# Retention attention into a mixture of experts: another order of the last attention tile, of its index load and scatters, and of the work behind them

## The chip, the cores and the metric

One NeuronCore of a Trainium2 chip runs the whole program in one launch. The metric is the device time of one execution in microseconds, the median over several executions. Shorter is better.

## What is computed

A block-wise retention attention over 4 sequences, 8 heads, 768 positions and 64 channels, whose output is regrouped into 3072 token rows of 512 numbers. Each row goes to one of 8 experts, the one with the largest gate logit.

```python
def _attn_ref(q, k, v, lam):
    ...
    for b in range(nb):
        ...
        intra = np.einsum('bhic,bhjc->bhij', qb, kb) * Dmask[None]
        intra = np.einsum('bhij,bhjd->bhid', intra, vb)
        inter = np.einsum('bhid,bhde->bhie', qb * lam_pow[None], kv_state)
        out[:, :, sl] = intra + inter
        kv_state = lam_block[None, :, None, None] * kv_state + np.einsum('bhsd,bhse->bhde', kb_dec, vb)

def _moe_ref(x, w_gate, w_output_gate, w1, w2):
    logits = x @ w_gate
    e_idx = np.argmax(logits, axis=1)
    ...
    for e in range(E):
        h = np.maximum(x[mask] @ w1[e], 0.0)
        out[mask] = gate_w[mask, None] * eom[mask, e, None] * (h @ w2[e])
```

## The kernel before

The attention part walks over 24 tiles (`NTILE`): 6 blocks of 128 positions by 4 sequences (`B`). `LAST` is 20, the first tile of the last block. Of each tile n, TensorE makes transposes of keys and queries (`pk`, `pq`), scores (`ps`, `stage_b`), the products of the scaled queries with the running state (`po`, `stage_c1`, line 424) and the products of the decayed scores `at` with the values, summed into the same `po` (`stage_c`, line 441). The scaled queries `qd` are made on GpSimd (line 375), in two halves for the last block. ScalarE copies `po` to `xT`, VectorE turns `xT` to token rows `xn` and SyncE writes them to the DRAM tensor `x_d` (`stage_d2`).

After each block of four tiles the gate logits are made (`logits`, `logit_rows`), VectorE chooses the expert (`route_choose`) and the place of each token in its expert's list (`route_place`), and GpSimd scatters a record of three numbers for each token to the DRAM table `tab_d` (`place_scatter`, one indirect DMA for each tile). Reading a list back (`load_rows`, the index) gives the rows to gather (`row_index`, then `gather`, one indirect DMA for 32 tokens, on GpSimd).

The expert part takes the experts by size, the first one (index 0 here) being picked early. Each expert's two weight matrices come in four pieces of 1 MB, 0 and 1 of `w1`, 2 and 3 of `w2`; piece 4 is the first of the next expert. `load_piece` issues one on SyncE's queue; there are three buffers, so a piece waits until the piece three before it has been split. A split makes a high part `whi` on ScalarE (`split_hi`) and a low part `wlo` on VectorE (`split_lo2`, line 146, two chunks of 128 rows at a time). Each product is the sum of three (`mm3`, lines 85 to 87).

The first expert's work starts while the last tiles are still being placed. Its first 192 rows (`FIRST`) are known early; its up products for them (`up_mm`, `ph`) and its down products (`down_rows_mm`, `pyr`) are cut into units, which `fill(count)` issues on TensorE between the steps of the last block. `settle` issues the activations that belong to units already made. Rows from place 352 on (`LATE`) belong to the last block's tokens; they aren't gathered but picked out of token rows on chip (`rows_of` transposes them, `mark_late` and `take_late` make the tile `chosen`, `split_late` splits it). Behind the units comes the second column half, `up(0, fc, 1)`, for columns 192 to 448, then the down products of the rest, then expert 1.

Instructions stand in the order in which the code is written, engine by engine, and each engine and each queue takes its own in that order. The waits between them are put in from the tiles that they share; DRAM tensors count as tiles.

## Time and profile before

| what | us |
|---|---|
| median of 3 runs | 416.05 (414.84 to 416.11) |
| the profiled execution: time | 415.14 |
| its span | 413.4 |
| TensorE busy in the span | 400.8 |
| VectorE, GpSimd, ScalarE busy | 286.7, 238.8, 190.4 |

The profile is that of one execution. Times in it are microseconds from the start of the span. The granted clock of TensorE is 1.00 of full speed in every stretch that is read here. TensorE's last products of the attention part start at 112.76, the first product of the experts at 116.83.

### The profile page before, as it was taken

Reading aid. Unit: us, or ns where it says so; the run is one execution under the profiler, and the core shown is the slowest. Engines: PE = TensorE matmul, PEld = TensorE weight load, DVE = VectorE, ACT = ScalarE, POOL = GpSimd, SP = SyncE. Lnnn points to the kernel's source line nnn. Section 1 sums busy time; section 2 is a strip of 40 time slices with the busy share of each in tenths; the row PEclk is TensorE's granted clock in tenths of the full one; section 3 lists DMA queues with packets and bytes.
Section 4 is the critical chain, followed back from the end, with each engine's and each line's share of the span. In section 5 each row is a group of like instructions: output and inputs, shape, how many; then the busy total and the mean of one; then the engine's idle time right before and its main releaser. Section 6 shows DMA issues by size and latency. Waiting matters only on the chain.

```text
span 413.4 us, 10570 instructions
## 1 busy us (share of the span) xinstructions
PE 400.8 (97%) x3869; PEld 367.1 (89%) x3869; DVE 286.7 (69%) x810; ACT 190.4 (46%) x460; POOL 238.8 (58%) x301
## 2 busy tenths in 40 slices
PE   7999999999899999999999999999999999999994
PEld 4889878798698698999999999999999989989983
DVE  2759697877888646876868857957965864873710
ACT  4767665665684033544145325504704543542400
POOL 5367679668846788674783665467386266120012
PEclk9999999999999999999999999999999999999999
DMA  8999898889972764544479548746846884461001
GB/s 177 231 254 246 226 258 224 215 230 259 322 231 79 222 206 144 170 141 135 150 209 297 198 135 241 262 178 200 292 140 186 295 271 151 127 224 46 5 27 52
DMA packets 95103, 79.11 MB, mean 191 GB/s; under 512 B 58445, under 2 KB 70769, under 8 KB 95041
## 3 DMA queue, kind: packets, MB, share of 16 engines
q1 hardware_dynamic: 88080, 64.88, 53.2%
q0 software_dynamic: 6240, 12.93, 10.0%
q8 instruction: 32, 0.52, 0.5%
q10 hardware_dynamic: 720, 0.53, 0.5%
q14 instruction: 31, 0.25, 0.2%
HBM read 62.25 MB, written 16.45 MB: 190 GB/s over the span
## 4 chain that ended last, share of the span: by engine, by line
PE 85%; DVE 6%; DMA 5%; issue 2%; POOL 1%; ACT 0%; POOLq 0%; DVEq 0%; SPq 0%
PE ph_None L86 10%; PE ph_None L87 10%; PE ph_None L85 10%; PE py L87 6%; PE py L86 6%; PE py L85 6%; PE pyr L86 5%; PE pyr L87 5%; PE pyr L85 5%; PE ps L400 4%; PE po L441 4%; PE pk L341 3%; PE po L424 2%; PE pq L341 2%; DVE at L409 2%; PE pst L454 2%
## 5 line engine op out<-in xcount | busy, mean ns | idle before, releaser
L900 POOL DMA_INDIRECT xg<-x_d,rows x100 | 110.6, 1106 | 54.8 <-issue 28.9
L1009 ACT ACTIVATE hhi<-ph_None 128x400 fp32r<-128x400 f32 (+4 forms) x56 | 28.1, 501 | 115.8 <-PE ph_None L87 111.0
L86 PE MATMUL ph_None<-xlo,whi 128*128 128x400 f32 (+4 forms) x224 | 76.2, 340 | 0.0
L87 PE MATMUL ph_None<-xhi,wlo 128*128 128x400 f32 (+4 forms) x224 | 76.1, 340 | 0.0
L85 PE MATMUL ph_None<-xhi,whi 128*128 128x400 f32 (+4 forms) x224 | 76.1, 340 | 0.0
L132 ACT CAST whi<-raw 128x512 fp32r<-128x512 f32 x128 | 74.7, 615 | 2.4 <-DMA raw<-in_moe_w_dram 2.4
L141 DVE TENSOR_TENSOR wlo<-raw,whi 128x512 fp32r<-128x512 f32 x112 | 74.5, 686 | 0.7 <-ACT whi L132 0.5
L1010 DVE SCALAR_TENSOR_TENSOR hlo<-ph_None,hhi 128x400 fp32r<-128x400 f32 (+4 forms) x56 | 31.9, 570 | 35.2 <-ACT hhi L1009 33.2
L87 PE MATMUL py<-hhi,wlo 128*128 128x400 f32 (+2 forms) x128 | 44.4, 347 | 0.0
L86 PE MATMUL py<-hlo,whi 128*128 128x400 f32 (+2 forms) x128 | 44.4, 347 | 0.0
L85 PE MATMUL py<-hhi,whi 128*128 128x400 f32 (+2 forms) x128 | 44.4, 347 | 0.0
L86 PEld LDWEIGHTS ph_None<-xlo,whi 128*128 128x128 f32 x224 | 42.0, 188 | 0.5 <-DVE xlo L935 0.2
L1126 POOL DMA_INDIRECT out_dram<-yn,table x12 | 12.5, 1045 | 51.8 <-DVE yn L1190 34.6
L85 PEld LDWEIGHTS ph_None<-xhi,whi 128*128 128x128 f32 x224 | 42.0, 188 | 0.4
L87 PEld LDWEIGHTS ph_None<-xhi,wlo 128*128 128x128 f32 x224 | 42.0, 188 | 0.2
L345 ACT COPY qT<-pq 64x256 f32<-64x256 f32 x96 | 37.8, 393 | 2.0 <-PE pq L341 1.0
L409 DVE TENSOR_TENSOR at<-ps,decay 128x512 f32<-128x512 f32 x48 | 31.1, 681 | 10.4 <-PE ps L400 10.4
L86 PE MATMUL pyr<-wlo,hhi 128*128 128x512 f32 (+2 forms) x96 | 37.8, 394 | 0.5 <-DVE wlo L146 0.5
L87 PE MATMUL pyr<-whi,hlo 128*128 128x512 f32 (+2 forms) x96 | 37.6, 391 | 0.0
L85 PE MATMUL pyr<-whi,hhi 128*128 128x512 f32 (+2 forms) x96 | 37.5, 390 | 0.0
L931 ACT CAST xhi<-y 128x256 fp32r<-128x256 f32 (+3 forms) x64 | 19.5, 357 | 31.5 <-DVE y L917 31.5
L679 POOL DMA_INDIRECT tab_d<-rec,idx x24 | 26.2, 1090 | 10.0 <-issue 4.1
(216 smaller groups left out, 783.0 us busy)
## 6 DMA issues: line engine op xcount, KB each, us to landing
raw<-in_moe_w_dram SPq DMA_DIRECT2D x32, 1024.0 KB
x_d<-xn SPq DMA_DIRECT2D x22, 256.0 KB
qkv<-in_k_dram SPq DMA_DIRECT2D x40, 128.0 KB
qkv<-in_v_dram SPq DMA_DIRECT2D x20, 256.0 KB
qkv<-in_q_dram SPq DMA_DIRECT2D x36, 128.0 KB
yd<-yo SPq DMA_DIRECT2D x12, 256.0 KB
yr<-yd SPq DMA_DIRECT2D x48, 64.0 KB
xg<-x_d,rows POOLq DMA_INDIRECT x100
```

Of the source, the lines that this page charges most:

```text
L85: nc.tensor.matmul(ps, a[0], b[0], start=first, stop=False)
L86: nc.tensor.matmul(ps, a[0], b[1], start=False, stop=False)
L87: nc.tensor.matmul(ps, a[1], b[0], start=False, stop=last)
L132: nc.scalar.copy(out=hi, in_=src)
L141: eng.tensor_tensor(out=lo, in0=src, in1=hi.bitcast(F32), op=ALU.subtract)
L341: nc.tensor.transpose(out=dst[:, m * P : (m + 1) * P], in_=src[:, m], identity=ident)
L345: copies = [lambda r=r, view=view, src=src: nc.scalar.copy(out=view(qT[r]), in_=src) for r, view, src in query_parts(pq)]
L409: nc.vector.tensor_tensor(out=at, in0=ps.rearrange("p (g t) -> p g t", g=NPAIR), in1=dec[:, j], op=ALU.mult)
L679: nc.gpsimd.indirect_dma_start(out=tab_d, out_offset=bass.IndirectOffsetOnAxis(ap=idx, axis=0), in_=rec, in_offset=None, bounds_check=P * ...
L900: nc.gpsimd.indirect_dma_start(out=xg[(p, i)][:, m * P : (m + 1) * P], out_offset=None, in_=x_q[0 : 4 * rows], in_offset=bass.IndirectOffs ...
L1009: nc.scalar.activation(out=hi[:, r], in_=ph[:, r], func=AF.Relu)
L1010: nc.vector.scalar_tensor_tensor(out=lo[:, r], in0=ph[:, r], scalar=0.0, in1=hi[:, r].bitcast(F32), op0=ALU.max, op1=ALU.subtract,)
```

## The change

All of it lies between the end of the attention part and the first expert. For the last tile (23) the products of scores and values go ahead of those of the state (`stage_last` in place of `stage_c1` and `stage_c`), and the row transposes of tiles 20 and 21 stand between the two, in banks of the tile's own scores. The up units start with columns 0 and 1 interleaved (first their first two input chunks, then the others), two units are issued ahead of the choice and six more behind it, eight ahead of the counts where there were four. The index load for the first expert's middle places moves from GpSimd to SyncE (`load_middle`, which reads only places below 352), and the last four scatters are declared free of it. Piece 3's load stands behind it on the queue. The first low half of piece 2 and `sort_rest` stand ahead of the first expert's second `row_index`; `stage_d2` of the last three tiles and `split_late` move behind the low parts of piece 3; piece 4's load stands ahead of the index of expert 1.

```diff
--- before.py
+++ after.py
@@ -297,6 +297,7 @@
         norow = wpool.tile([P, E * EB * 3], I32, tag="raw", bufs=3, name="norow")
         nc.gpsimd.memset(norow, NOROW)
         nc.sync.dma_start(tab_d.rearrange("(p r) t -> p (r t)", p=P), norow)
+        nc.gpsimd.memset(middle_t, NOROW)
 
 
     later = []
@@ -404,7 +405,8 @@
     def stage_b2(n):
         L = live[n]
         dec = decay.rearrange("p (y m) t -> p y m t", y=2)
-        for j, ps in enumerate(L.pop("ps")):
+        L["kept"] = L.pop("ps")
+        for j, ps in enumerate(L["kept"]):
             at = slot(f"at_{n}_{j}").rearrange("p (g t) -> p g t", g=NPAIR)
             nc.vector.tensor_tensor(
                 out=at, in0=ps.rearrange("p (g t) -> p g t", g=NPAIR), in1=dec[:, j], op=ALU.mult
@@ -428,6 +430,39 @@
                             start=(i == 0),
                             stop=False,
                         )
+
+    def stage_last(n, between):
+        L = live[n]
+        b = n % B
+        vt = qkv[n][2]
+        ps = L["kept"]
+        L["po"] = [bank(f"po_{n}_{y}") for y in range(2)]
+        for y in range(2):
+            for m in range(4):
+                i, j = divmod(m, 2)
+                nc.tensor.matmul(
+                    L["po"][y][j * D : (j + 1) * D, i * P : (i + 1) * P],
+                    vt[:, 4 * y + m, :],
+                    L["at"][y][:, m, :],
+                    start=(i == 0),
+                    stop=False,
+                )
+        copies = between(ps)
+        for i in range(2):
+            for y in range(2):
+                for j in range(2):
+                    r = slice(y * D, (y + 1) * D)
+                    nc.tensor.matmul(
+                        L["po"][y][j * D : (j + 1) * D, i * P : (i + 1) * P],
+                        state[b][r, 2 * i + j, :],
+                        L["qd"][r, 2 * i + j, :],
+                        start=False,
+                        stop=(i == 1),
+                    )
+        xT = L["xT"] = xTs[n] = slot(f"xT_{n}")
+        for y in range(2):
+            nc.scalar.copy(out=xT[:, 256 * y : 256 * y + 256], in_=L["po"][y][:, 0:256])
+        return copies
 
     def stage_c(n):
         L = live[n]
@@ -488,9 +523,10 @@
     spaces = {}
     xTs = {}
 
-    def logits(n0, nb):
+    def logits(n0, nb, pl=None):
         parts = P // EG // nb
-        pl = bank(f"pl_{n0}")
+        if pl is None:
+            pl = bank(f"pl_{n0}")
         for i in range(NPAIR // parts):
             for b in range(nb):
                 xTv = xTs.pop((n0 + b)) if i == NPAIR // parts - 1 else xTs[n0 + b]
@@ -671,20 +707,23 @@
 
     pending = []
 
-    def place_scatter(count):
+    def place_scatter(count, beside=()):
         for _ in range(min(count, len(pending))):
             idx, rec = pending.pop(0)
-            scatter(
-                "table",
-                nc.gpsimd.indirect_dma_start(
-                    out=tab_d,
-                    out_offset=bass.IndirectOffsetOnAxis(ap=idx, axis=0),
-                    in_=rec,
-                    in_offset=None,
-                    bounds_check=P * E * EB - 1,
-                    oob_is_err=False,
-                ),
-            )
+            ins = nc.gpsimd.indirect_dma_start(
+                out=tab_d,
+                out_offset=bass.IndirectOffsetOnAxis(ap=idx, axis=0),
+                in_=rec,
+                in_offset=None,
+                bounds_check=P * E * EB - 1,
+                oob_is_err=False,
+            )
+            scatter("table", ins)
+            for other in beside:
+                tc.declare_no_dep(
+                    getattr(ins, "ins", ins), other,
+                    reason="the first expert's places below LATE are read, the last tiles' places begin at LATE",
+                )
 
     def scatter(group, ins):
         inst = getattr(ins, "ins", ins)
@@ -834,6 +873,18 @@
         eng.dma_start(t, src.rearrange("e (b r) j t -> (e r) b (j t)", b=4))
         idxs[(p, j0)] = (t, n)
 
+    middle_t = const.tile([32, 4, 2, 3], I32, name="index_0_1")
+
+    def load_middle():
+        parts = []
+        idxs[(0, 1)] = (middle_t, 2)
+        for j in range(2):
+            nb = min(4, (LATE - P * (j + 1)) // 32)
+            src = tab_v[bass.ds(expert[0], 1)][:, 0 : 32 * nb, 1 + j : 2 + j, :]
+            ins = nc.sync.dma_start(middle_t[:, 0:nb, j, :], src.rearrange("e (b r) j t -> (e r) b (j t)", b=nb))
+            parts.append(getattr(ins, "ins", ins))
+        return parts
+
     def load_outs(p, j0=0, j1=None):
         if p >= E:
             return
@@ -941,13 +992,14 @@
 
     token_rows = {}
 
-    def rows_of(n):
+    def rows_of(n, pt=None):
         xT = live[n]["xT"]
-        pt = bank(f"pt_{n}")
+        if pt is None:
+            pt = bank(f"pt_{n}")
         for g in range(NPAIR):
             nc.tensor.transpose(out=pt[:, g * P : (g + 1) * P], in_=xT[:, g * P : (g + 1) * P], identity=ident)
         t = token_rows[n] = slot(f"xr_{n}")
-        nc.scalar.copy(out=t, in_=pt)
+        return lambda: nc.scalar.copy(out=t, in_=pt)
 
     chosen = []
 
@@ -1194,10 +1246,11 @@
 
     units = []
     acts = []
-    for fc in range(NFC):
-        for kc in range(NKC):
-            act = (lambda fc=fc: up_act(0, fc, 0)) if kc == NKC - 1 else None
-            units.append((lambda fc=fc, kc=kc: up_mm(0, fc, 0, kc), act))
+    for fc, kc in [(f, c) for h in range(2) for f in range(2) for c in (2 * h, 2 * h + 1)] + [
+        (f, c) for f in range(2, NFC) for c in range(NKC)
+    ]:
+        act = (lambda fc=fc: up_act(0, fc, 0)) if kc == NKC - 1 else None
+        units.append((lambda fc=fc, kc=kc: up_mm(0, fc, 0, kc), act))
     for j in range(2):
         for fc in range(NFC):
             act = (lambda j=j: emit_rows(0, j, phs.pop((0, "y", j)))) if fc == NFC - 1 else None
@@ -1344,33 +1397,34 @@
         for f in held[6:]:
             f()
         place_scatter(B)
-        load_rows(0, 1, 3, nc.gpsimd)
+        middle = load_middle()
         stage_c(n - 1)
         for g in range(NPAIR):
             x_hi(0, g, 0)
         for g in range(NPAIR):
             x_lo(0, g, 0)
         split_lo2(0, 0)
+        load_piece(3)
+        copies = stage_last(n, lambda free: [rows_of(LAST + i, free[i]) for i in range(2)])
+        pl = bank("pl_last")
+        copies.append(rows_of(LAST + 2))
         split_hi(0, 2)
-        load_piece(3)
-        stage_c1(n)
-        stage_c(n)
         split_hi(0, 3)
         split_lo2(0, 1)
-        for i in range(2):
-            rows_of(LAST + i)
-        logits(LAST, B)
-        rows_of(LAST + 2)
+        logits(LAST, B, pl)
+        copies.append(rows_of(LAST + 3))
+        for f in copies[:3]:
+            f()
         for j in range(2):
             split_hi(1, j)
+        copies[3]()
+        fill(2)
         logit_rows(LAST)
         choose = route_choose(LAST, NTILE)
-        at_once(choose[:-1])
-        rows_of(LAST + 3)
-        choose[-1]()
+        at_once(choose)
         for j in range(2, 4):
             split_hi(1, j)
-        fill(4)
+        fill(6)
         place = route_place(LAST, NTILE)
         counts = rank_counts("pcount")
         place[0]()
@@ -1381,32 +1435,34 @@
         fill(4)
         take_late(LAST)
         at_once(place[4:])
-        place_scatter(B)
+        place_scatter(B, middle)
         settle()
         for h in range(2):
             split_lo2(1, h)
         for j in range(4):
             split_hi(2, j)
+        split_lo2(2, 0)
+        sort_rest(counts)
         row_index(0, 1)
         gather(0, 6, 11, LAST * P)
-        stage_d2(LAST + 1)
-        stage_d2(n - 1, 2)
-        split_late()
-        sort_rest(counts)
         expert_regs(1, order_i[:, 1:2], 1)
+        load_piece(4)
         load_rows(1)
-        load_piece(4)
         load_outs0()
         expert_regs(2, order_i[:, 2:E], E - 2)
         for h in range(2):
             split_hi(3, 2 * h)
             split_hi(3, 2 * h + 1)
             fill(8)
-            split_lo2(2, h)
             settle()
+            if h == 0:
+                split_lo2(2, 1)
         for h in range(2):
             split_lo2(3, h)
             fill(2)
+        stage_d2(LAST + 1)
+        stage_d2(n - 1, 2)
+        split_late()
         row_index(1)
         gather(1, 0, 4)
         settle()
```

On TensorE, the last tile's products before: `po_23` are the two halves of the output of tile 23, `pt` the transposed rows, `pl` the logits, `at` the decayed scores.

```order
L424 MATMUL po_23_0_2599<-qkv_23_1_2119,state_1_140 64x128 x2
L424 MATMUL po_23_1_2600<-qkv_23_1_2119,state_1_140 64x128 x2
L424 MATMUL po_23_0_2599<-qkv_23_1_2119,state_1_140 64x128 x2
L424 MATMUL po_23_1_2600<-qkv_23_1_2119,state_1_140 64x128 x2
L441 MATMUL po_23_0_2599<-at_23_0_2536,qkv_23_1_2119 64x128 x4
L441 MATMUL po_23_1_2600<-at_23_1_2538,qkv_23_1_2119 64x128 x4
L948 MATMUL pt_20_2622<-ident_101,xT_20_2396 128x128 x4
L948 MATMUL pt_21_2629<-ident_101,xT_21_2493 128x128 x4
L501 MATMUL pl_20_2636<-xT_20_2396,wgs_107 32x128
```

The same place with the change:

```order
L443 MATMUL po_23_0_2600<-at_23_0_2538,qkv_23_1_2121 64x128 x4
L443 MATMUL po_23_1_2601<-at_23_1_2540,qkv_23_1_2121 64x128 x4
L1000 MATMUL ps_23_0_2520<-ident_101,xT_20_2398 128x128 x4
L1000 MATMUL ps_23_1_2521<-ident_101,xT_21_2495 128x128 x4
L455 MATMUL po_23_0_2600<-qkv_23_1_2121,state_1_140 64x128 x2
L455 MATMUL po_23_1_2601<-qkv_23_1_2121,state_1_140 64x128 x2
L455 MATMUL po_23_0_2600<-qkv_23_1_2121,state_1_140 64x128 x2
L455 MATMUL po_23_1_2601<-qkv_23_1_2121,state_1_140 64x128 x2
L1000 MATMUL pt_22_2632<-ident_101,xT_22_2570 128x128 x4
L537 MATMUL pl_last_2631<-xT_20_2398,wgs_107 32x128
```

The four rows with `state` have moved behind the score products and behind the transposes of `xT_20` and `xT_21`.

On SyncE's queue, from the write of tile 20's rows (`xn_20`) to piece 5, before (`raw` are pieces, `index_1` and `table_0` read `tab_d`, the `ISA` rows set registers):

```order
L534 DMA x_d_72<-xn_20_2475 128x512
...
L119 DMA raw_3_2597<-in_moe_w2_dram 128x4x512
L534 DMA x_d_72<-xn_21_2839 128x512
L534 DMA x_d_72<-xn_22_2842 128x2x512
L738 TENSOR_LOAD order_i_152
L738 ISA x2
...
L834 DMA index_1_0_2870<-tab_d_73 32x4x12
...
L119 DMA raw_4_2872<-in_moe_w1_dram 128x4x512
...
L738 TENSOR_LOAD order_i_152
L738 ISA x12
...
L119 DMA raw_5_3048<-in_moe_w1_dram 128x4x512
```

And with the change:

```order
L570 DMA x_d_72<-xn_20_2477 128x512
...
L884 DMA index_0_1_157<-tab_d_73 32x4x3
...
L884 DMA index_0_1_157<-tab_d_73 32x3x3
...
L119 DMA raw_3_2598<-in_moe_w2_dram 128x4x512
L777 TENSOR_LOAD order_i_152
L777 ISA x2
...
L119 DMA raw_4_2873<-in_moe_w1_dram 128x4x512
...
L873 DMA index_1_0_2875<-tab_d_73 32x4x12
...
L777 TENSOR_LOAD order_i_152
L777 ISA x12
L570 DMA x_d_72<-xn_21_3026 128x512
L570 DMA x_d_72<-xn_22_3029 128x2x512
```

Piece 3 now stands behind two index loads, and the writes of tiles 21 to 23 (`xn_21`, `xn_22`) behind piece 4, the index of expert 1, the tables and the second register load.

On VectorE, from the low parts of piece 1 on, before:

```order
L146 TENSOR_TENSOR wlo_1_2663<-raw_1_2299,whi_1_2662 128x1024 x2
L869 SCALAR_TENSOR_TENSOR rowf_0_1_2815<-index_0_1_2566 32x8
L874 TENSOR_SCALAR rows_0_1_2817<-rowf_0_1_2815 32x8 x4
L532 STREAM_TRANSPOSE xn_21_2839<-xT_21_2493 128x512
L532 STREAM_TRANSPOSE xn_22_2842<-xT_22_2568 128x512
L532 STREAM_TRANSPOSE xn_22_2842<-xT_23_2609 128x512
...
L146 TENSOR_TENSOR wlo_2_2810<-raw_2_2411,whi_2_2809 128x1024
...
L146 TENSOR_TENSOR wlo_2_2810<-raw_2_2411,whi_2_2809 128x1024
...
L146 TENSOR_TENSOR wlo_3_2934<-raw_3_2597,whi_3_2933 128x1024 x2
L869 SCALAR_TENSOR_TENSOR rowf_1_0_3024<-index_1_0_2870 32x16
L874 TENSOR_SCALAR rows_1_0_3026<-rowf_1_0_3024 32x16 x4
```

And with the change:

```order
L146 TENSOR_TENSOR wlo_1_2669<-raw_1_2301,whi_1_2668 128x1024 x2
L146 TENSOR_TENSOR wlo_2_2827<-raw_2_2413,whi_2_2826 128x1024
...
L920 SCALAR_TENSOR_TENSOR rowf_0_1_2839<-index_0_1_157 32x8
L925 TENSOR_SCALAR rows_0_1_2841<-rowf_0_1_2839 32x8 x4
...
L146 TENSOR_TENSOR wlo_2_2827<-raw_2_2413,whi_2_2826 128x1024
...
L146 TENSOR_TENSOR wlo_3_2937<-raw_3_2598,whi_3_2936 128x1024 x2
L568 STREAM_TRANSPOSE xn_21_3026<-xT_21_2495 128x512
L568 STREAM_TRANSPOSE xn_22_3029<-xT_22_2570 128x512
L568 STREAM_TRANSPOSE xn_22_3029<-xT_23_2628 128x512
```

The transposes to `xn` have moved from ahead of `wlo_2` to behind `wlo_3`, and the index `rowf_0_1` from ahead of them to behind the first half of `wlo_2`.

## Rows read from the trace of the kernel before

**Rows 1.** Timeline of TensorE, 124 to 145: start us, us, operation [idle before <-releaser]

```profile
124.76 0.34 PE L85 MATMUL ph<-xhi,whi 128*128 128x192 f32 x1
...
131.52 0.41 PE L85 MATMUL pyr<-whi,hhi 128*128 128x512 f32 x1
...
132.43 0.50 PE L86 MATMUL pyr<-wlo,hhi 128*128 128x512 f32 x1 [0.49 <-DVE wlo L146]
...
144.18 0.28 PE L85 MATMUL ph<-xhi,whi 128*128 128x256 f32 x1
```

**Rows 2.** Chain of waits, 164 to 169: start us, us, what

```profile
166.58 0.23 PE pyr L87
166.80 0.20 PE ph_None L85
167.00 0.34 PE ph_None L86
```

**Rows 3.** Timeline of TensorE, 110 to 117

```profile
110.40 0.45 PE L424 MATMUL po<-qkv,state 64*64 64x128 f32 x8
...
112.38 0.45 PE L424 MATMUL po<-qkv,state 64*64 64x128 f32 x8 [1.53 <-POOL qkv L375]
...
116.83 0.33 PE L85 MATMUL ph<-xhi,whi 128*128 128x192 f32 x1
```

**Rows 4.** Timeline of VectorE, two places

```profile
122.63 0.18 DVE L634 RECIPROCAL rec<-pr 128x4 f32<-128x4 f32 x1
...
164.90 1.14 DVE L917 STREAM_TRANSPOSE y<-xg 128x512 f32<-128x512 f32 x2 [2.78 <-DMA xg<-x_d,rows]
```

**Rows 5.** Timeline of GpSimd, 113 to 164

```profile
114.11 1.13 POOL L679 DMA_INDIRECT tab_d<-rec,idx  x1 [0.59 <-issue]
...
115.54 1.97 POOL L679 DMA_INDIRECT tab_d<-rec,idx  x1 [0.30 <-issue]
...
119.08 0.97 POOL L679 DMA_INDIRECT tab_d<-rec,idx  x1 [0.30 <-issue]
...
131.63 1.59 POOL L679 DMA_INDIRECT tab_d<-rec,idx  x1 [0.30 <-issue]
...
133.53 1.44 POOL L900 DMA_INDIRECT xg<-x_d,rows  x1 [0.30 <-issue]
...
140.80 0.99 POOL L900 DMA_INDIRECT xg<-x_d,rows  x1 [0.30 <-DMA xg<-x_d,rows]
```

**Rows 6.** GpSimd's gathers by line, 140.5 to 163.5

```profile
L900 POOL DMA_INDIRECT xg<-x_d,rows x14 | 14.7, 1050 | 3.1 <-issue 2.8 <-DMA xg<-x_d,rows 0.3
```

**Rows 7.** VectorE's low parts by line, 122.6 to 138.3

```profile
L146 DVE TENSOR_TENSOR wlo<-raw,whi 128x1024 fp32r<-128x1024 f32 x6 | 7.1, 1219 | 0.0
```

**Rows 8.** Timeline of SyncE's queue, 116 to 141

```profile
116.69 0.38 SPq L119 DMA_DIRECT2D raw<-in_moe_w_dram  x1
...
128.47 1.55 SPq L534 DMA_DIRECT2D x_d<-xn  x2
...
134.41 0.36 SPq L834 DMA_DIRECT2D index<-tab_d  x1
...
135.60 1.85 SPq L852 DMA_DIRECT2D table<-tab_d  x3
...
140.60 0.38 SPq L119 DMA_DIRECT2D raw<-in_moe_w_dram  x1
```

**Rows 9.** Windows: busy us by engine (count), clock, DMA share, GB/s

```profile
118.50:121.50 3.00, 3.00 (x33) 3.00 (x31) 2.46 (x13) 1.96 (x7) 1.24 (x2) 1.00 0.96 313
...
122.60:138.30 15.70, 15.20 (x105) 12.92 (x103) 14.31 (x38) 5.61 (x16) 10.19 (x11) 1.00 0.30 95
...
129.00:132.00 3.00, 2.93 (x26) 2.62 (x24) 2.86 (x13) 1.00 (x4) 2.31 (x3) 1.00 0.73 262
```

**Rows 10.** Chain of waits, 110 to 133

```profile
119.08 4.78 DMA tab_d<-rec,idx
```

**Rows 11.** Timeline of ScalarE, 119 to 130

```profile
125.54 1.17 ACT L132 CAST whi<-raw 128x512 fp32r<-128x512 f32 x2
```

## Prediction

> **What bounds the kernel now.** I read the chain of waits backwards from the end, then TensorE's timeline, then the queues that feed it. From 144.18, where the second column half of the first expert begins, TensorE works without a wait to the last rows, with one exception, at 167.00 [rows 1, 2]. So a gain must move 144.18, and it is kept only if the exception moves with it.
>
> Ahead of 144.18 TensorE idles at two places. In the last attention tile the state's products wait 1.53 us for GpSimd's second half of the scaled queries (110.40 to 112.38) [rows 3]. From 131.52 to 144.18, 48 products of 0.23 us would take 11.0, and took 12.7 [rows 1, 2]: four waits, all for VectorE, the first 0.49 for the low part of piece 2, and three more like it: 1.7 us in all.
>
> The exception is the reader's second place to look. The first up-product of expert 1 takes 0.34 us where its neighbours take 0.20, since it waits for `xlo` [rows 2]. Behind that stands VectorE, which waited 2.78 us for the last gather before it transposed at 164.90 [rows 4]; and behind the gather stands GpSimd, whose 14 gathers for expert 1 run back to back from 140.80 to 163.5, with little but issue gaps between them (2.8 of 3.1 us idle are "issue") [rows 5, 6]. So two chains arrive at 167 almost together: TensorE's own, and GpSimd's queue from 140.80. The smaller gain of the two counts.
>
> **The change, TensorE's side.** The last tile's value products and eight transposes go ahead of the state's products, so the 1.53 is filled. The work from 110.40 to 116.83 is 6.43 with the wait, 4.9 without [rows 3]: units begin at about 115.3. Eight units (0.34 each, as the 20 from 124.76 to 131.52 took [rows 1]) come before the counts instead of four, and end at 118.1. The counts need the choice of experts, which VectorE makes behind its own queue (low parts of piece 0), and nothing of that moves: they stay at about 118.2. Up to the end of the `chosen` products (124.76) time is as before, but four units more are done: 1.34 gained. Then a new wait: the fifth unit group now comes directly behind `chosen` and needs the second low half of piece 1, which VectorE ends near 126.0 (the reciprocal at 122.7 [rows 4], four small subtractions of some 0.25, two of 1.2 [rows 7]); TensorE is there near 125.7: 0.4 lost. The remaining four groups end at 124.7 + 0.2 + 5.4 + 0.4 = 130.6. The down products then find their low parts early if piece 3 is in time: 130.6 + 11.0 = 141.6 in place of 144.18, a gain of **2.6**. The gathered rows for that moment, which TensorE needs 2.6 sooner, come from gathers that start near 130 instead of 133.53 [rows 5], 3.5 sooner, so they stay hidden.
>
> **GpSimd's side.** Its index load, which waited until 123.86 and held the queue behind it, goes to SyncE, and the last four scatters no longer wait for that load. VectorE's reciprocal ends at 122.81 [rows 4], 0.1 sooner now; GpSimd needs some 0.7 (0.59 idle "issue" ahead of the same step at 114.11 [rows 5]): first scatter 123.4, four of 0.97 with gaps of 0.31: 128.2. From below that is the bound. From above: scatters that ran beside a low-part subtraction took 1.97 and 1.59 instead of 0.97 [rows 5], and the new place lies beside three subtractions of 1.2 us [rows 7]; two such scatters at 0.6 each give 129.5, my value. The second group of before ended at 133.22 and its landing released SyncE at 134.41, 1.2 later [rows 5, 8]: landing at 130.7.
>
> The Trainium skill, page "SBUF — State Buffer", section "Who interferes with whom", speaks against the new place: a VectorE instruction with two SBUF inputs blocks a GpSimd instruction that reads SBUF for its whole length. By that rule three scatters could lose up to 1.2 each, and the sum would lose its gain; the trace's 1.97 and 1.59 agree in kind.
>
> **What the gathers of expert 1 wait for.** They read the last three tiles' rows, so those must be in DRAM. Their transposes (`xn`) move behind the low parts of piece 3, and their writes move on SyncE's queue behind piece 4, the index of expert 1, three tables and twelve register loads. In before the index left at 134.41, the tables began two issues and 1.2 later (so 0.6 without piece 4 between) and took 1.85, and the next load after the registers left at 140.60 [rows 8]. So now: index 130.7, tables 131.3 to 133.15, registers to 136.3, first write 136.3, second 137.05. In before the second write left near 129.65, and the traffic was over by 132 [rows 8, 9]: 2.35, and 0.4 for receipt and release. Gathers of expert 1: **139.8** (139.1 without the slow scatters) in place of 140.80. VectorE isn't the later one: of its 14.31 busy us in 122.60 to 138.30 [rows 9] all but late low parts and the last index (1.8) now lie ahead of the write, so the transposes end near 122.7 + 12.5 = 135.2.
>
> **The new wait at SyncE.** Its index loads now wait for the first scatters, and piece 3 is queued behind them. Piece 3 left at 116.69 [rows 8]; now it leaves 1.3 after the scatters land. In before they landed 4.78 after issue at 119.08 [rows 10], while piece 3 itself filled the DMA (313 GB/s in 118.5 to 121.5 [rows 9]); that cover of traffic is gone now. Bounds: 121.3 (1.2 after the scatter's end, as unloaded) to 123.9. I take 121.5, being unloaded: issue 122.8. A 1 MB piece took 5.0 (116.69 to 121.7): landed at 127.8. Behind it on ScalarE are two casts (1.17 [rows 11]) and two activations, then VectorE's low parts of them near 129.0; piece 3 is free up to about 127.3, and with SyncE's later queue up to about 129.2.
>
> **Sum.** TensorE could gain 2.6, but expert 1's gathers begin only 1.0 to 1.7 sooner: I take 1.2, and the other 1.4 comes back as a wait of TensorE at the first up-product of expert 1. The profiled execution took 415.14 (span 413.4, 1.7 around it); the three runs' median is 416.05, their lowest 414.84. From 415.6, between the two, 414.4. A change below 0.3% (1.25) can't be told from none here, so the forecast lies on that edge.
>
> **Rivals.** (a) *Forecast*: gathers start at 139.0 to 140.2, 0.6 to 1.8 gained, 414.4. Chance 0.47; about 0.30 of it beyond the edge.
> (b) *Full gain*: SyncE's register loads or the writes are quicker than I add up, gathers start by 138.4, and TensorE's 2.6 is the limit: 413.0. For it: each step of SyncE's sum is a loaded one. Against it: five steps in a row. Chance 0.17.
> (c) *Gain lost at the old gate*: the scatters are blocked by three subtractions (up to 3.6) or land late, gathers start at 140.2 to 142.0: 0.6 gained to 1.2 lost, about 415.9, no change. TensorE is early at 164 and waits there 2 to 3 us. The skill's rule just named would do this. For it: the 1.97. Against: the gather at 133.53, beside such a subtraction, took 1.44 against 0.99 at 140.80, 0.45 more only [rows 5]. Chance 0.26.
> (d) *Slower*: piece 3 is late. If the scatters land at 123.9 as before and the piece takes longer than 5.2, it lands past 130.2, ScalarE holds the activations behind its casts, VectorE holds low parts and transposes, and gathers start after 140.80. From there each us costs one; beyond 131.5 it shows as slower. At 132: 1.8 lost, 417.4. Against: there is no other traffic then. Chance 0.10.
>
> Faster 0.30 + 0.17 = 0.47, same 0.17 + 0.26 = 0.43, slower 0.10. The range reaches from (b) less the runs' spread, 412.5, to (c) and a little of (d), 416.3; the forecast's own is 413.6 to 415.2.
>
> **What would show it.** Right: no GpSimd wait in the last tile's products; the second column half starts at 141.6; first scatter of the last group near 123.4; piece 3 issued near 122.8; second `x_d` write near 137; a gap on GpSimd of 2 to 4 us ahead of expert 1's first gather at 139.8; TensorE waits more than 1 us for `xlo` near 164 to 166. Wrong: the second half starts later than 142.5 (low parts or piece 3), or TensorE has no wait at expert 1 (then (b)), or another wait downstream that before doesn't show.

## The result and the profile after

The change made the kernel slower: 420.35 us median over 22 runs against 416.67 for the kernel before (22 runs beside them), a ratio of **1.008, 95% interval [1.0056, 1.0104]**, some 3.3 us. The profiled execution took 419.77 (span 418.1); before's took 415.14 (span 413.4). Ratios leave out disturbed executions, which the medians include (so 3.3 and not 3.7), and one experiment's profile (piece 5 later) is of such an execution, so only distances within it are used.

Of the 4.7 us between the two profiled executions a part has nothing to do with the change. The last tile's decay multiplication, which stands ahead of every instruction that the change moves (but for one small memset), comes 2.69 later: 112.21 here, 109.52 in before. TensorE had waited 4.4 us for the attention part's keys (1.1 in before's trace, in the same view). From here on a time "in before's clock" is one of this trace less 2.69.

VectorE's timeline of the kernel before and after, 108 to 115, and TensorE's waits up to 110 in each (us in total, times, longest):

```profile
109.52 1.25 DVE L409 TENSOR_TENSOR at<-ps,decay 128x512 f32<-128x512 f32 x2
112.21 1.25 DVE L411 TENSOR_TENSOR at<-ps,decay 128x512 f32<-128x512 f32 x2
```

```profile
PE pk L341 <- DMA qkv<-in_k_dram: 1.1, 2, 0.7
PE pk L342 <- DMA qkv<-in_k_dram: 4.4, 4, 1.5
```

TensorE's side came as forecast. In its timeline the wait of 1.53 us for GpSimd [rows 3] is gone, and the second column half starts at 144.47, 141.78 in before's clock, against 144.18 [rows 1]:

```profile
112.92 1.35 PE L443 MATMUL po<-at,qkv 128*64 128x128 f32 x16 [0.40 <-DVE at L411]
114.20 1.09 PE L1000 MATMUL ps<-ident,xT 128*128 128x128 f32 x8
115.22 0.67 PE L455 MATMUL po<-qkv,state 64*64 64x128 f32 x16
...
133.44 0.41 PE L85 MATMUL pyr<-whi,hhi 128*128 128x512 f32 x1
...
144.47 0.28 PE L85 MATMUL ph<-xhi,whi 128*128 128x256 f32 x1
...
169.89 0.47 PE L85 MATMUL ph_None<-xhi,whi 128*128 128x432 f32 x1 [2.09 <-ACT xhi L982]
```

The last line is where it is lost. Expert 1's first up-product waits 2.09 us for its tokens and starts at 169.89; in before it was the 0.20 at 166.80 with a 0.34 behind it [rows 2] (a chain shows only the part of a product behind the one ahead; in the timeline that product starts at 166.64, which the distances below use). The gathers that bring these tokens explain it. GpSimd's timeline: the four scatters are early, the five middle gathers follow at once, and then it stands 5.34 us before expert 1's first gather, at 144.68 (before: 140.80, back to back [rows 5]):

```profile
126.31 1.04 POOL L713 DMA_INDIRECT tab_d<-rec,idx  x1 [3.05 <-issue]
127.66 2.02 POOL L713 DMA_INDIRECT tab_d<-rec,idx  x1 [0.30 <-issue]
129.99 0.97 POOL L713 DMA_INDIRECT tab_d<-rec,idx  x1 [0.30 <-DVE wlo L146]
131.26 0.97 POOL L713 DMA_INDIRECT tab_d<-rec,idx  x1 [0.31 <-issue]
...
138.34 0.99 POOL L951 DMA_INDIRECT xg<-x_d,rows  x1 [0.30 <-issue]
144.68 0.99 POOL L951 DMA_INDIRECT xg<-x_d,rows  x1 [5.34 <-PE pyr L87]
```

The releaser named (TensorE) isn't the one: the gather waits for several semaphores (the counters by which one engine or transfer releases another), and its row numbers were ready at 140.26. SyncE's queue tells which: the two `x_d` writes that the gather reads left at 139.16 and 139.6, with piece 5 (1 MB) directly behind. In the trace's semaphore updates the second write is complete at 143.91, 0.77 ahead of the gather's start. The same 0.76 to 0.77 stands between the two in the four experiments that keep the late writes (a1, e5, e8, e9 below), and e5's row names the write.

```profile
123.92 0.91 SPq L884 DMA_DIRECT2D index<-tab_d  x2
125.40 6.88 SPq L119 DMA_DIRECT2D raw<-in_moe_w_dram  x2
133.84 0.33 SPq L873 DMA_DIRECT2D index<-tab_d  x1
134.36 1.83 SPq L903 DMA_DIRECT2D table<-tab_d  x3
139.16 0.83 SPq L570 DMA_DIRECT2D x_d<-xn  x2
140.25 0.39 SPq L119 DMA_DIRECT2D raw<-in_moe_w_dram  x1
```

The DMA was idle up to 140 and then full (windows: busy us by engine, clock, DMA share, GB/s). The 768 KB of the writes share it with piece 5:

```profile
139.00:140.00 1.00, 1.00 (x6) 0.62 (x5) 0.94 (x7) 0.00 (x0) 0.34 (x1) 1.00 0.02 4
140.00:141.00 1.00, 1.00 (x6) 0.54 (x4) 0.96 (x3) 0.00 (x0) 0.00 (x0) 1.00 0.91 287
...
144.00:145.00 1.00, 1.00 (x8) 0.85 (x7) 0.33 (x1) 0.00 (x0) 0.32 (x1) 1.00 0.97 340
```

Behind 170 the two traces run in step, 3.41 apart, to the last rows; the remaining 1.3 is the landing of the very last scatter (5.5 us from its end to the end of the span here, 4.2 in before). So of the 4.7, 2.69 lie ahead of the changed code, 0.7 in it and 1.3 behind it: this one pair of executions shows where the gathers hold, but only 0.7 of the median's 3.3 us.

### The profile page after: what moved, and what is told of

It is laid out like the page before. It is cut to its first block, busy times and chain, and to the rows that moved or that the text cites. A ratio compares the mean times of both kernels' runs of the same rounds, so it can differ in the third digit from the quotient of the medians.

```text
span 418.1 us, 10574 instructions
## 1 busy us (share of the span) xinstructions
PE 399.8 (96%) x3869; PEld 366.5 (88%) x3869; DVE 286.5 (69%) x810; ACT 190.2 (45%) x460; POOL 235.7 (56%) x301
## 4 chain that ended last, share of the span: by engine, by line
PE 81%; DVE 7%; DMA 6%; POOL 2%; issue 2%; ACT 1%; SPq 0%; POOLq 0%; DVEq 0%; ACTq 0%
PE ph_None L85 10%; PE ph_None L86 10%; PE ph_None L87 10%; PE py L87 6%; PE py L85 6%; PE py L86 6%; PE pyr L86 4%; PE pyr L85 4%; PE pyr L87 4%; PE ps L401 4%; PE po L476 3%; PE pk L342 2%; DMA qkv<-in_k_dram 2%; DVE at L411 2%; PE po L426 2%
## 5 line engine op out<-in xcount | busy, mean ns | idle before, releaser
L951 POOL DMA_INDIRECT xg<-x_d,rows x100 | 109.0, 1090 | 63.8 <-issue 33.3
```

The source lines that it names most:

```text
L951: nc.gpsimd.indirect_dma_start(out=xg[(p, i)][:, m * P : (m + 1) * P], out_offset=None, in_=x_q[0 : 4 * rows], in_offset=bass.IndirectOffs ...
```

## The experiments

They ran in four sets (e1 to e4; a1 and e5 to e7; e8 to e11; e12 and e13), each on one chip with the kernel before beside it; a ratio is always to those runs. The sets' medians of before were 424.19, 424.21, 423.79 and 416.78, so times of different sets aren't compared. The five sets of this study (with that of the result, where before has 416.67) thus fall into two where before takes 417 us (the 417 sets) and three where it takes 424 (the 424 sets).

**Theories.** A: the late `x_d` writes hold expert 1's gathers, and these hold TensorE. B: what came early in the trace (the 2.69) is the change's doing. C: piece 4, now ahead of expert 1's index on SyncE, delays that index. D: TensorE's order and the index on SyncE lose by themselves.

**Only the memset** (e1). To the kernel before:

```diff
+        nc.gpsimd.memset(middle_t, NOROW)
...
+    middle_t = const.tile([32, 4, 2, 3], I32, name="index_0_1")
```

> The kernel before, with nothing added but the constant tile of the middle index (96 bytes a partition) and GpSimd's 0.1 us memset of it in blank_rows; no index is read into it. Theory A (the 2.7 us by which the changed kernel's trace was late at tile 23's kT, before anything that the change moves, are variation of the transfers of one execution): 416.7 us, ratio 0.998 to 1.002, and kT of tile 23 anywhere from 103 to 108 us. Theory B (the tile and the memset disturb the transfers of the attention part in every execution): 418.5 to 420 us, ratio 1.005 to 1.008, TensorE waiting 3 us or more for in_k_dram as in the changed kernel's trace (4.4 us against 0).

Measured: 0.9974 [0.9946, 1.0001], not slower. B falls. Its multiplication of the last tile came at 114.04; in 15 of the 16 traces of this study it lay between 109.5 and 114.8, and before's 109.52 is the earliest of all (the next is 112.21). The attention part varies by more than the change is worth.

**TensorE's order alone** (e3: stage_last, the four copies, the unit order and the fill counts in the kernel before).

> The kernel before with TensorE's part of the change alone: stage_last with the row transposes, the four copies, the unit order of the pyr products and the fill counts; the index stays on GpSimd, the scatters keep their wait, the x_d writes their place. Theory A (the gain of TensorE's order is real, but the chain of expert 1's gathers holds): the second column half starts 2 to 2.6 us sooner than 144.18, expert 1's first up-product starts where it did (167.0 relative to tile 23's scores) behind a wait of 2 to 2.9 us, time 416.0 to 416.7, ratio 0.998 to 1.000. Rival (TensorE's order itself costs): later than 144.18, ratio over 1.003.

Measured: 0.9993 [0.9964, 1.0021]. It neither costs nor gains. The gain of the second half, expected at 2 to 2.6, did not show here: it starts 36.73 behind the last tile's decay multiplication (34.66 in before's trace of the first set), since TensorE waits 2.4 us for VectorE's low parts within the down products, which in this kernel are not moved.

**The index on SyncE with free scatters alone** (e4, and again as e10).

```diff
...
-        load_rows(0, 1, 3, nc.gpsimd)
+        middle = load_middle()
...
-        place_scatter(B)
+        place_scatter(B, middle)
```

> The kernel before with the middle index read by SyncE into its constant tile and the last scatters free of it, and nothing else. Theory A (variation early on; the gathers of expert 1 move up by some 3 us, but TensorE was only 0.34 us behind them): 416.2 to 416.7 us, ratio 0.998 to 1.001. Theory B (the tile disturbs the attention part): 418.5 to 420. Rival (piece 3, issued on SyncE behind the index, arrives late: TensorE or VectorE waits for raw of piece 3 past 130.2 us): 417.4 to 419, with whi of piece 3 waiting 2 us or more beyond what before's shows.

> The kernel before with the index on SyncE and the free scatters alone, a second time and beside the others. If its 0.9951 was a gain: 0.992 to 0.998. If it was the spread between runs (the kernel with only the memset gave 0.9974): 0.998 to 1.002.

Measured: 0.9951 [0.9923, 0.9979], then 0.9985 [0.996, 1.001]. Not slower, perhaps a little faster; the first number, outside the 0.998 to 1.001 expected, was in part spread.

**Both, with the tail as before** (e7, and again as e11).

> The kernel before with TensorE's order and the index on SyncE with the free scatters, and the program from the last scatters on (low parts, token rows, sort, piece 4) exactly as before. Theories A and C (the loss is in the order of the tail): ratio 0.993 to 0.999, as index alone (0.9951) and TensorE alone (0.9993) add up. Rival D (the two lose together): 1.003 or more.

> The kernel before with TensorE's order, the index on SyncE and the free scatters, the tail as before, a second time. If these parts gain: 0.992 to 0.998, at or below the index alone. If TensorE's order adds nothing to the index: the same as the index alone within 0.003. If nothing gains: 0.998 to 1.002.

Measured: 0.9972 [0.9939, 1.0005] and 0.9977 [0.9946, 1.0008]. D falls: what loses is in the tail. This is the version to keep, though neither interval alone excludes no change. TensorE's second half starts 35.47 and 35.57 behind the last decay multiplication here, no sooner than in before's trace: the down products ahead of it wait 0.75 and 0.40, the second wait named for a low part.

**The token rows put back ahead of the sort** (e2), in the changed kernel:

```diff
         split_lo2(2, 0)
-        sort_rest(counts)
         row_index(0, 1)
         gather(0, 6, 11, LAST * P)
+        stage_d2(LAST + 1)
+        stage_d2(n - 1, 2)
+        split_late()
+        sort_rest(counts)
...
-        stage_d2(LAST + 1)
-        stage_d2(n - 1, 2)
-        split_late()
```

> The changed kernel with the last three tiles' token rows (stage_d2 twice and split_late) put back where they stood, behind the middle gathers and ahead of sort_rest. Theory A (the two x_d writes, issued at 139.16 and landed about 144.4 beside piece 5, hold expert 1's gathers, and these hold TensorE's first product of expert 1 by 2.1 us): the gathers start right behind the middle ones (5.34 us of waiting at 144.68 gone, at most 1 us left), the 2.1 us wait of the up-products of expert 1 goes, and the time falls by 2.1 us from the changed kernel's 420.35 to 418.2, or further, to 415.3, if the early lateness was variation. Rival (the gathers are not what holds; the scattered index or the tables follow as the next wait): the gathers still start 3 us or more behind the middle ones and the time stays at 419.5 to 420.5.

Measured: 1.0029 [0.9997, 1.0061]; no wait at expert 1 is left. But the gathers still stood 2.26 us: with the sort behind the transposes, the index left SyncE late (139.15, behind piece 4) and was read at 143.79. That was the sign of C.

**Changed kernel again, piece 4 put back, and piece 4 with the token rows put back** (a1, e5, e6), on one chip. e5 is the first diff alone, e6 has both:

```diff
+        load_rows(1)
         load_piece(4)
-        load_rows(1)
```

```diff
         gather(0, 6, 11, LAST * P)
+        stage_d2(LAST + 1)
+        stage_d2(n - 1, 2)
+        split_late()
...
-        stage_d2(LAST + 1)
-        stage_d2(n - 1, 2)
-        split_late()
```

> The changed kernel once more, on the chip that also runs the next three, so that they can be set against it. The earlier runs gave a ratio of 1.008 [1.0056, 1.0104]; theory A (order of the tail) and its rivals all expect 1.005 to 1.010 here.

> The changed kernel with piece 4's load put back behind expert 1's index and table loads on SyncE, where it stood. Theory C (the 1 MB of piece 4, now ahead, delays the index load of expert 1 behind it: issued 139.15, read at 143.79 in the run with the token rows put back, 4.6 us, where before's took less): the index lands 2 us or more sooner, but the x_d writes still hold the gathers: ratio 1.003 to 1.008. Theory A alone (only the x_d writes matter): 1.006 to 1.010, as the changed kernel. Rival: piece 4 later costs a wait of VectorE or ScalarE on raw: above 1.010.

> The changed kernel with both put back: the last token rows right behind the middle gathers (but behind sort_rest, which stays ahead), and piece 4 behind expert 1's index and tables. What is left of the change: TensorE's order, the index on SyncE with free scatters, low parts of piece 2 ahead of the sort. Theories A and C together: the loss goes, and the scatters' head start shows: ratio 0.993 to 0.999, expert 1's gathers straight behind the middle ones. Rival D (TensorE's order and the index lose together, apart from the tail): 1.003 or more.

Measured: 1.0101 [1.0063, 1.0138]; 1.011 [1.0075, 1.0145]; 1.0003 [0.9969, 1.0037]. Between e5 and e6 the place of the token rows (transposes, writes and `split_late`) is the only difference, and it is worth 1.1%. Piece 4 alone changes nothing while the writes are the later wait. In e6 the gathers follow the middle ones with 0.71 us between; the gain expected of it (0.993 to 0.999) did not come. One chip shows both ends of the move: the second half starts 33.75 and 33.78 behind the last decay multiplication in a1 and e5, 35.45 in e6. TensorE's gain and the late writes are one exchange on VectorE's queue. GpSimd's timeline of e5:

```profile
146.72 0.99 POOL L951 DMA_INDIRECT xg<-x_d,rows  x1 [3.73 <-DMA x_d<-xn]
```

**The late writes alone, in the kernel before** (e8): the three lines moved behind the low parts of piece 3.

> The kernel before, with one move: the last tiles' token rows (stage_d2 twice and split_late) go behind the low parts of piece 3, where the change puts them. Theory A (their late x_d writes alone make the loss, by way of expert 1's gathers): expert 1's gathers start 3 us or more behind the middle ones, TensorE waits or stands still before expert 1's first up-product, ratio 1.006 to 1.011. Rival (the late writes hurt only together with TensorE's new order or the index on SyncE): 0.998 to 1.003.

Measured: **1.0119 [1.0082, 1.0156]**. The one move makes a loss as large as the whole change's, without the rest of it. It moves `split_late` too, but TensorE's second half starts 33.97 behind the last decay multiplication, and no wait there is named for what that makes. GpSimd stands 5.53 us there:

```profile
141.23 0.99 POOL L900 DMA_INDIRECT xg<-x_d,rows  x1 [0.30 <-issue]
147.76 0.99 POOL L900 DMA_INDIRECT xg<-x_d,rows  x1 [5.53 <-DVE yn L1190]
```

**Piece 5 held back** (e9), so that the writes have the DMA to themselves:

```diff
-        gather(1, 0, 4)
+        gather(1, 0, 1)
+        raws[5] = wpool.tile([P, 4, 512], F32, tag="raw", bufs=3, name="raw_5")
+        nc.gpsimd.memset(raws[5][:, 0, 0:1], 0.0)
+        gather(1, 1, 4)
         settle()
         load_piece(5)
```

> The changed kernel with piece 5 held back: GpSimd writes one element of its buffer (0.1 us) right behind expert 1's first gather, so that SyncE can issue the 1 MB only once the x_d writes have landed. Theory A1 (the writes are late because piece 5 shares the transfers with them: 768 KB took 4 to 5 us from issue to gather): the first gather comes 2.0 to 2.8 us behind the second write's issue instead of 3.9 to 5.1, ratio 1.003 to 1.007. Theory A2 (the writes' place behind the low parts is what costs, the sharing adds little): the first gather stays 3.5 us or more behind the issue, ratio 1.008 to 1.012.

Measured: 1.0092 [1.0062, 1.0123]. From the second write's issue to the gather 3.67 us, against 5.08 in the changed kernel's first trace, and 4.28, 3.88 and 4.78 in a1, e5 and e8. A2 is nearer: sharing adds 0.2 to 1.4, and without it the writes still take a microsecond more than I allowed. The semaphore updates divide it: in e9 the second write is complete 2.91 behind its issue, and the gather starts 0.77 later. Before and e12, where no large load leaves until it is complete, show 2.90 and 2.83 for the same write; e5, a1, e8 and the changed kernel, where piece 5 leaves 0.6 to 0.8 behind, 3.12, 3.51, 4.02 and 4.31. Windows of e9: the traffic lasts to 154, the gather starts at 154.94.

```profile
151.00:152.00 1.00, 1.00 (x6) 0.54 (x5) 0.13 (x2) 0.00 (x0) 0.46 (x1) 1.00 0.65 229
152.00:153.00 1.00, 1.00 (x6) 0.59 (x5) 0.61 (x1) 0.00 (x0) 0.00 (x0) 1.00 1.01 334
153.00:154.00 1.00, 1.00 (x6) 0.62 (x5) 0.00 (x0) 0.00 (x0) 0.00 (x0) 1.00 0.81 309
154.00:155.00 1.00, 1.00 (x6) 0.54 (x4) 0.31 (x1) 0.27 (x2) 0.06 (x1) 1.00 0.00 0
```

**Late gathers with early writes** (e12): e7 with GpSimd kept busy ahead of expert 1's first gather.

```diff
+        for _ in range(24):
+            nc.gpsimd.iota(held_t, pattern=[[1, 4]], base=0, channel_multiplier=1)
         gather(1, 0, 4)
```

> The kernel before with TensorE's order and the index on SyncE, the writes of the token rows early (0.9972 and 0.9977 before), and 24 small iotas of GpSimd into an unused tile (0.12 to 0.15 us each, some 3 us) ahead of expert 1's first gather. Theory A (the late gathers are the road: TensorE comes to expert 1 before its tokens, its clock falls): ratio 1.006 to 1.012, the gathers 3 us later, TensorE standing still or waiting 2 us or more before expert 1's first up-product, clock 0.5 for some us. Rival (the late gathers alone are hidden; the order on VectorE and SyncE of the late writes is what costs): 0.997 to 1.002.

Measured: 1.0093 [1.0058, 1.0127], where the same kernel without the iotas had 0.9972 and 0.9977, on two other chips. They took longer than I put (4.75 us). The wait at expert 1 is the changed kernel's to a hundredth, by chance: both the gathers and the second half start later here (34.19 and 34.64 behind the last decay multiplication, against 32.47 and 32.26). That second half starts where it does in before's trace (34.66, of the first set), so the iotas don't delay it; expert 1's first up-product then comes 3.04 behind before's, for gathers 2.91 later. The clock stayed at 1.00, which theory A had not expected. So late gathers are enough for a loss of this size; that the order of VectorE's and SyncE's queues matters in no other way isn't shown. GpSimd's timeline of e12, then TensorE's:

```profile
141.09 4.75 POOL L1467 IOTA held<- 128x4 int32 x24
146.65 1.02 POOL L952 DMA_INDIRECT xg<-x_d,rows  x1 [0.81 <-DVE yn L1243]
```

```profile
172.62 0.47 PE L85 MATMUL ph_None<-xhi,whi 128*128 128x432 f32 x1 [2.10 <-ACT xhi L983]
```

**Only the token rows put back, behind the sort** (e13: the second diff of e6 alone).

> The changed kernel with the token rows' transposes and writes alone put back behind the middle gathers (behind sort_rest); piece 4 stays ahead of expert 1's index and tables, the low parts stay early. Theory A (the writes are the whole loss): 0.996 to 1.003, as with piece 4 put back too (1.0003). Theory C (piece 4 ahead delays expert 1's index, 4.6 us from issue to use in an earlier run): 1.004 to 1.008.

Measured: 1.0053 [1.0023, 1.0083], as C has it. With the writes early, the index is the next wait. It leaves 0.6 behind piece 4's 1 MB, VectorE has it 6.1 us later after a wait of 2.93, and GpSimd stands 3.54. Timelines of e13, of SyncE's queue, VectorE and GpSimd:

```profile
135.15 0.39 SPq L119 DMA_DIRECT2D raw<-in_moe_w_dram  x1
135.78 0.36 SPq L873 DMA_DIRECT2D index<-tab_d  x1
```

```profile
141.87 0.17 DVE L920 SCALAR_TENSOR_TENSOR rowf<-index 32x16 f32<-32x16 int32 x1 [2.93 <-DMA index<-tab_d]
```

```profile
143.51 0.99 POOL L951 DMA_INDIRECT xg<-x_d,rows  x1 [3.54 <-issue]
```

The late index is shown, its price only by the ratio: e13's gathers start where before's do (31.26 and 31.28), and its trace comes to expert 1 0.57 sooner than before's.

So the tail held two delays, the second hidden by the first. Putting back the second alone (e5) is worth nothing, the first alone (e13) removes a third to a half of the loss (on another chip), both remove it.

All traces side by side, in us from the last tile's decay multiplication (worked out from one profiled execution each, so good to 1 to 2 us: e4 and e10 are the same kernel):

```
                        ratio    2nd x_d write   expert 1's 1st gather   1st up-product
before                  1        20.13           31.28                   57.12
changed                 1.0080   27.39           32.47                   57.68
e12 gathers held        1.0093   20.37           34.19                   60.17
e13 token rows back     1.0053   21.63           31.26                   56.55
(the three 424 sets)
e7  tail as before      0.9972   20.79           30.14                   59.04
e11 the same            0.9977   20.86           30.22                   59.25
e10 index only          0.9985   19.77           30.91                   60.43
e6  both put back       1.0003   22.66           30.13                   59.00
e9  piece 5 held        1.0092   29.25           32.92                   64.09
e5  piece 4 back        1.0110   29.30           33.18                   63.81
a1  changed             1.0101   29.27           33.55                   64.59
e8  late writes only    1.0119   30.15           34.93                   64.80
e1  memset only         0.9974   19.66           29.47                   60.54
e2  token rows early    1.0029   21.87           31.66                   60.53
e3  TensorE only        0.9993   20.91           31.20                   59.88
e4  index only          0.9951   22.74           33.74                   62.35
```

No trace of before was kept on the other chips; e1, which is before with a memset, stands in for it there. The e4 trace is not on the line (a late gather with the lowest ratio); its profiled execution lay 2 us above its own median, and the same kernel's second trace (e10) is on it.

What the first gather of expert 1 waits for comes out of these traces: it starts 0.76 to 0.77 us behind the second write's completion (changed, a1, e5, e8, e9), or 0.74 behind VectorE's last row number (e2, e3, e4, e6, e7, e10, e11, e13), or directly behind GpSimd's own work (before, e1, e12). What it costs is less clear. In the 417 sets the changed trace loses 0.56 at expert 1's first up-product and e13's gains 0.57, where the ratios say 3.3 and 2.2 us lost, so the traces don't hold the whole price; in the 424 sets the first up-product and the ratio go together (a1 against e7, on one chip: 5.5 us by either).

## Why the prediction was wrong

The range (412.5 to 416.3) started from 415.6, between one profile and three runs. The 22 runs of before beside the change have a median of 416.67, so the base was 1.1 too low, and the upper end lay below the kernel before itself. That is apart from the sign, which was wrong too.

In before's clock, step by step:

- **TensorE's gain: right.** Second half forecast at 141.6, measured 141.78. The new waits were 0.40 (for the decay multiplication, not foreseen) and 0.22 (low part, put at 0.4). But e3, e6 and e7 show that the gain hangs on the low parts being early: TensorE's new order alone doesn't bring it.
- **Scatters: right.** First at 123.4, measured 123.62; the four done at 129.5, measured 129.54. One of the four took 2.02. By the rule of the Trainium skill ("SBUF — State Buffer", "Who interferes with whom"), that a VectorE instruction with two SBUF inputs contends with a GpSimd instruction that reads SBUF, the prediction's estimate was that up to 3.6 us could be lost; 1.1 was.
- **Piece 3: right.** Issued at 122.8, measured 122.71. ScalarE's cast, which waited for it, began at 130.98, so it landed near 128.3; I had 127.8, free up to 129.2. Rival (d) did not come.
- **Second `x_d` write: right.** 137.05 forecast, 136.9 measured.
- **The step that failed** is the next: "2.35, and 0.4 for receipt and release", from the second write's issue to expert 1's gathers at 139.8. They started at 141.99, 2.2 later. I read 2.35 off coarse windows of before, and gave the writes an empty DMA although piece 5 leaves SyncE directly behind them. The changed kernel took 5.08 for these 2.75. The excess has three parts: the same write took 2.90 in before's own trace and not 2.35 (0.55), the gather starts 0.77 behind its completion and not 0.4 (0.37), and with piece 5 beside it the write took 1.41 more. e9, without piece 5, shows 3.67. The gathers thus start 1.2 later than in before, not 1.0 sooner, and TensorE's gain comes back as a wait at expert 1: the mechanism was named, the size had the wrong sign.
- **The price of a late gather** was put at one for one: rival (c) put gathers at 142.0 to 1.2 us. The traces of the two 417 sets don't speak against it: the changed kernel's gathers start 1.19 later than before's and its first up-product 0.56, e12's 2.91 and 3.04. But the ratios have 3.3 and 3.9 us. For the first chip this stays open: its one trace accounts for 0.6 to 0.7 us only. On a1's chip the price is higher in the rows too: against e7 a1 starts its gathers 3.4 later, its first up-product 5.5 later, and loses 1.3% (5.5 us). There TensorE doesn't wait for tokens at all; it stands still in the second half and its clock falls (below), which the prediction had nothing of.
- **Hidden behind it, not foreseen:** piece 4 ahead of expert 1's index. I counted its issue, not that a 3 KB load behind 1 MB is itself late (e13). In the changed kernel itself it cost nothing: VectorE read the index without a wait, and the writes came later.

## What to carry to other kernels

A write to DRAM that a later gather reads is a link of that gather's chain: price it from issue to the reader's start beside the traffic that will leave right behind it, not by the traffic's end in a quiet stretch (here 3.7 us alone and up to 5.1 beside a 1 MB load, where 2.75 was taken). Where two chains arrive together, moving work ahead on the one by putting the other's work behind it gave nothing here, and a small load behind a large one in its queue came late (6.1 us in e13). Undo single moves in pairs: with two delays in a row, taking back one showed nothing.

## What the runs showed of the hardware

In the four profiles with late writes in the three 424 sets (a1, e5, e8, e9) TensorE hardly waits at expert 1 (0.16 in e8, nothing in the others), but stands still in expert 0's second half (in e8 also in the down products behind it), mostly in steps of 1.40 to 1.46 us with no releaser named: in a1 at 157.73, 159.19, 160.59, 162.02, 163.46 and 164.87. They come to 3.4 to 4.4 us of idle time a trace; the other kernels of these sets show 0 to 0.8 there, e1 and e2 some 2, and the traces of the two 417 sets none. The 96 products of that half take 11.4 us from the first start to the last in the 417 sets, 11.4 to 14.2 in the 424 sets with early writes, and 17.9 to 18.6 in a1, e5 and e9. TensorE's timeline of a1, and windows of it:

```profile
157.73 0.28 PE L87 MATMUL ph<-xhi,wlo 128*128 128x256 f32 x1 [0.38 <-issue]
159.19 0.36 PE L86 MATMUL ph<-xlo,whi 128*128 128x256 f32 x1 [0.70 <-issue]
160.59 0.29 PE L86 MATMUL ph<-xlo,whi 128*128 128x256 f32 x1 [0.81 <-issue]
```

```profile
153.00:156.00 3.00, 3.00 (x28) 3.00 (x27) 0.43 (x1) 0.38 (x1) 2.39 (x3) 1.00 0.37 126
156.00:159.00 3.00, 2.11 (x17) 1.81 (x15) 0.00 (x0) 0.00 (x0) 2.53 (x4) 1.00 0.34 87
159.00:162.00 3.00, 1.01 (x5) 0.98 (x6) 0.42 (x1) 0.38 (x1) 2.68 (x6) 1.00 0.15 44
162.00:165.00 3.00, 1.45 (x7) 1.39 (x7) 0.00 (x0) 0.10 (x1) 1.18 (x2) 0.68 0.16 44
165.00:168.00 3.00, 3.00 (x11) 2.62 (x11) 2.60 (x6) 2.37 (x6) 1.87 (x4) 0.50 0.00 0
168.00:171.00 3.00, 3.00 (x11) 2.36 (x10) 3.00 (x8) 2.31 (x7) 2.83 (x4) 0.68 0.16 44
171.00:174.00 3.00, 3.00 (x15) 2.47 (x14) 2.89 (x10) 0.85 (x2) 1.59 (x3) 1.00 0.64 152
```

Behind these stand-stills the granted clock (the column ahead of the DMA share) is 0.50, the 1.2 GHz level, in the window from 165, and back at 1.00 only in that from 171; the down products there take 0.63 instead of 0.39. All timed runs of a1 and e5 show a mean clock of 0.986 to 0.991, before's beside them 0.990 to 0.998.

ScalarE's rows show that the stand-still is only the end of something. An activation follows each twelve products. In the 417 sets the first seven of the eight start 0.04 us behind the last product's end, one each 1.44. In all twelve traces of the 424 sets, whatever the kernel, some start later, at the most by 2.0 (e10) to 6.0 us (e2) with early writes and by 8.8 to 10.7 with late ones. In the timeline of e5 they are 4.3 apart, three times the usual distance, and its waits end with TensorE's semaphore:

```profile
150.96 0.39 ACT L1061 ACTIVATE hhi<-ph 128x256 fp32r<-128x256 f32 x1 [1.27 <-PE ph L87]
155.23 0.38 ACT L1061 ACTIVATE hhi<-ph 128x256 fp32r<-128x256 f32 x1 [3.88 <-PE ph L87]
159.54 0.38 ACT L1061 ACTIVATE hhi<-ph 128x256 fp32r<-128x256 f32 x1 [3.92 <-remote]
163.83 0.38 ACT L1061 ACTIVATE hhi<-ph 128x256 fp32r<-128x256 f32 x1 [3.91 <-PE ph L87]
```

So in the 424 sets TensorE's completions reach ScalarE late in every kernel, and late gathers go with more of it. What holds them, and why more beside late gathers, stays open: no run here tells it. It may be part of why the kernel before takes 416.7 us in two sets (the first runs and e12's) and near 424 in the other three; against before's trace e1's has 4.5 more in the attention part, 3.4 between it and expert 1, and 1.3 behind.
